# New instruction orders for all engines of a four-layer attention and gated-MLP kernel, with the loads in another order

## The chip, the cores and the metric

The kernel runs on one core of one Trainium2 chip. The metric is the device time of one execution in microseconds (us). One launch runs the whole program: two attention layers and two gated layers, alternating, with the activations kept in on-chip memory from the first load to the last store.

## The reference

The input x is 1 x 2048 x 448 in bf16. Cut to what matters, this is computed:

```python
def A(x, wqkv, wo):                       # 16 heads of 28
    q, k, v = split_heads(x @ wqkv)
    idx = pos[:, None] - (arange(8) * 2)[None, :]     # 8 keys, every second position back
    logits = where(idx >= 0, einsum("bhsd,bhswd->bhsw", q, k[idx]) * 28 ** -0.5, -1e9)
    o = einsum("bhsw,bhswd->bhsd", softmax(logits), v[idx])
    return merge_heads(o) @ wo

def B(x, w_gate, w_up, w_down):           # 448 -> 1792 -> 448
    return ((x @ w_gate) * (x @ w_up)) @ w_down

x = x + A(layernorm(x), A_wqkv, A_wo)
x = x + B(layernorm(x), B_w_gate, B_w_up, B_w_down)
x = x + A(layernorm(x), A_wqkv, A_wo)
x = x + B(layernorm(x), B_w_gate, B_w_up, B_w_down)
```

## The kernel before

**Tiling.** Tokens lie in 16 blocks of 128, even positions in blocks 0 to 7 and odd ones in 8 to 15, so that the dilated window of 8 becomes a plain window of 8 neighbours. A layer is cut into chunks: layer 0 into chunks of 256, 512, 512, 512 and 256 tokens (blocks 0-1, 2-5, 6-9, 10-13, 14-15), the others likewise. `SEQ` (line 99) gives the order in which attention chunks (A) and gated chunks (B) are set up.

**Operations.** `build` adds 1592 numbered operations to a `Sched`. Each has the engines that may run it, its instructions, the keys it waits for and the PSUM banks that it takes or gives back. The number is the order in which `build` adds them, and the same number means the same operation before and after the change. What the text below names:

- 0 and 1 load the two halves of the first x block group (blocks 0-1 and 2-3), 6, 11 and 12 the other x groups (four blocks each); 7 and 8 load the V weights, 2 to 5 the four row pieces of the Q and K weights into a staging area, 9 and 10 the V columns that later ride in the padding of the Q and K weights (all in `load_x` and `plain_dma`, line 440).
- 13 loads ScalarE's function table; 14 (`c_warm`) clears the operand of the warm-up products, 16 (`c_wo`) clears `wo_g`.
- 46 to 61 are 16 warm-up products that keep TensorE busy with zeros.
- 62 to 69 copy the staged Q and K weights into `WQK` with each head padded from 28 to 32 columns (line 518); 70 to 77 fill the padding with V columns (line 526), which may only be done when the Q and K products of chunks 0 and 1 are finished.
- 99 to 196 are layer 0's layer norm, for each block B: statistics (line 579), aggregate (581), logarithm and exponential on ScalarE (582, 584), the normalised block `xn` (600), its transpose on TensorE (610, 614), and the copy `T` out of PSUM into `xnTa` (621, 624).
- 197 to 208 are Q and K of chunk 0 and their copies (line 709), 227 to 238 those of chunk 1, 349 to 360, 495 to 506 and 570 to 579 those of chunks 2, 3 and 4. 209 to 212 are V of query block 0, 239 to 242 V of query blocks 1 and 2, and so on.
- Scores S (832), their exponential (841), mask (848), the attention product AV (866), its copies and normalisation (877 to 904), and the output product Y (in `y_blocks`), whose result is added to x (921), are for one or two query blocks at a time: 214, 219 for block 0; 248, 253 for blocks 1 and 2; 270, 275 for 3 and 4; and so on.
- In a gated chunk, 14 units of gate and up products (`Gps`, `Ups`) are followed by a copy of the gate on ScalarE (957) and the product of both on VectorE (960); two passes of down products (`Dd`) follow, and the result is added to x.

**Products in halves.** The 448-deep products are cut in pieces of 64 rows; two pieces run at once in the two row halves of the array. `crossed` cuts a unit in two parts: in the second part the two outputs change row halves, and it waits for the first part's last product (`selfd`). Other units stand between the parts in the order, or none.

**Bursts.** S and AV are 64 (for query block 0, 32) short products in tiles of 64 x 32. An entry `248*2/350` in the order of TensorE says that operation 248 is cut in three, and two steps of unit 350 stand in between, each as eight products of 32 columns (line 350); the rest of 350 follows.

**The order.** Nothing is decided at run time. `ORDER` (line 101) lists, for each engine, the operations in the order in which they are issued; `BANKS` says which of the eight PSUM banks each operation takes. `Sched.schedule` reads both, and adds a wait for the operation that gives a bank back. `emit` writes one instruction stream for each engine, with a semaphore wait only where an operation needs another engine's result or a DMA. "sp" is the queue on which nearly all DMAs are issued, in order; a DMA that waits holds back all behind it. ScalarE issues two of the first loads on its own queue.

The few lines of the old order that matter here (the beginning of each list):

```python
"pe":  "46 ... 61 108 111 203 201 204 199 129 202 200 126 209 197 210 135 198 239 132 240 231 ..."
"act": "4 13 5 63 62 67 101 105 102 106 109 112 117 118 208 123 124 207 127 206 136 205 ..."
"dve": "14 16 44 15 45 99 103 100 104 64 65 68 107 110 113 115 114 116 121 119 128 ..."
"sp":  "7 0 3 8 10 2 11 9 1 6 12 79 80 78 81 82 ..."
```

So the loads go out as V weights, half of x, a Q and K piece, V weights, and so on, with two Q and K pieces on ScalarE's queue beside them; VectorE copies three of the Q and K weight pieces ahead of the first normalised block; and TensorE begins with Q and K of chunk 0.

Of the kernel before, what the change touches and what calls it, by code (L numbers as in the profile page):

```python
# [93 lines left out]
def grp_nc(g):  # L94
# [8 lines left out]
        "46 47 48 49 50 51 52 53 54 55 56 57 58 59 60 61 108 111 203 201 204 199 129 202 200 126 209 197 210 135 198 239 132 240 231 233 232 229 234 156 230 "  # L103
        "174 159 227 214 228 183 195 192 153 219 150 570 574 571 353 575 177 349 354 248*2/350 351 352 355 568 356 253*3/569 243 180 244 495 368 496 270*2/369 "
        "265 499 266 500 275*2/572 372 573 373 501 378 502 497 498 287 288 383 514 304 515 307 310 316 328 319 331 395 301 396 313 325 337 322 334 340 343 "
        "400*3/344 345 525*3/346 441 444 450 405*2/453 530*2/456 468 480 465 417 477 418 587 542 462 543 474 588 447 547*2/459 471 519 489 520 490 598*3/483 "
        "491 552*2/492 664 676 603*2/484 688 670 682 694 485 486 592 615 593 616 661 620*2/673 685 697 667 625*2/700 754 564 755 565 735 758 736 759 737 741 "
        "738 742 637 739 638 740 679 691 828 703 764*1/704 825 705 706 837 778*2/840 709 710 849 783+769*3/711 712 895 822 834 846 858 896 976 897 917 898 918 "
        "988 1000 852 979 819 893 899 894 900 985 795 997 1012 1009 991 1003 1015 796 912 831 843 855 982 994 913 867 868 1018 923*3/869 870 861 928*2/862 1006 "
        "863 864 1019 1034 945*3/1020 1046 940 1021 950*2/941 1058 1070 1043 1037 1040 1123 1108 1124 1109 1106 962 1107 963 1049 1061 1073 1128 1055 1129 1110 "  # L110
        "1104 1111 1105 1052 1064 1067 1076 1077 1134*2/1197 1078 1079 1209 1156*2/1206 1218 1275 1279 1276 1280 1139*2/1200 1161*2/1294 1212 1224 1281 1295 "
        "1282 1203 1215 1151 1173 1221 1233 1152 1230 1299 1174 1300 1227 1277 1236 1278 1247 1248 1239 1249 1310*3/1250 1240 1401 1395 1407 1398 1404 1241 "
        "1332*3/1242 1419 1315*2/1413 1337*2/1431 1304 1425 1416 1428 1327 1410 1328 1422 1349 1434 1350 1445 1446 1305 1437 1354*3/1438 1447 1448 1439 "
        "1359*2/1440 1476 1488 1473 1485 1371 1497 1509 1372 1479 1491 1503 1482 1494 1506 1500 1512 1544 1556 1515 1516 1541 1553 1565 1517 1518 1550 1523 "
        "1524 1547 1559 1571 1562 1574 1568 1580 1577 1525 1526 1589 1583 1586"
    ),
    "act": (
        "4 13 5 63 62 67 101 105 102 106 109 112 117 118 208 123 124 207 127 206 136 205 133 241 242 147 189 148 190 165 237 166 141 171 238 172 236 160 142 "
        "216 215 235 184 221 151 577 579 178 224 359 249 250 225 358 360 255 576 181 262 258 263 259 503 272 271 370 371 505 276 277 295 578 296 374 284 280 "
        "285 281 379 380 504 506 385 384 305 425 516 426 308 392 388 311 389 393 317 320 329 332 302 314 326 431 323 432 338 335 341 402 401 527 526 442 445 "  # L120
        "451 719 720 406 407 454 532 414 457 410 415 411 469 539 481 540 535 466 536 478 463 645 646 475 589 448 548 651 460 652 549 472 521 600 599 553 554 "
        "665 561 557 562 558 677 877 689 878 671 612 683 613 608 695 609 594 725 726 662 621 622 809 674 810 686 698 668 627 626 701 634 756 635 630 631 743 "
        "760 803 804 744 680 692 970 829 971 766 765 826 838 779 883 841 884 780 850 770 785 788 789 823 835 1088 1089 774 847 775 859 902 792 977 793 919 989 "
        "1001 853 980 820 904 986 998 1013 1010 992 1004 1016 832 1028 1029 844 856 983 914 995 924 925 1259 1260 1007 933 937 934 938 1035 946 1094 947 1095 "
        "1047 951 952 1059 1044 955 1071 1038 956 1041 959 960 1181 1125 1182 1114 1113 1265 1266 1050 1062 1074 1187 1056 1188 1130 1115 1053 1065 1068 1136 "
        "1135 1198 1210 1157 1158 1207 1219 1283 1140 1201 1162 1144 1145 1148 1213 1149 1166 1167 1225 1170 1286 1171 1204 1216 1222 1234 1231 1379 1301 1380 "
        "1228 1237 1385 1386 1311 1312 1402 1396 1408 1399 1405 1334 1333 1420 1317 1414 1338 1324 1339 1325 1320 1432 1321 1426 1346 1347 1417 1342 1429 1343 "
        "1411 1423 1457 1435 1458 1306 1463 1464 1356 1355 1361 1360 1477 1364 1368 1365 1369 1489 1474 1486 1498 1510 1480 1492 1535 1536 1504 1483 1495 1507 "
        "1501 1513 1545 1557 1542 1554 1566 1551 1548 1560 1572 1563 1575 1569 1581 1578 1588"
    ),  # L130
    "dve": (
        "14 16 44 15 45 99 103 100 104 64 65 68 107 110 113 115 114 116 121 119 128 120 122 125 130 137 131 134 163 145 169 164 187 146 161 185 138 143 186 170 "
        "144 188 167 162 139 155 140 158 168 211 213 173 157 212 175 182 191 194 149 152 218 72 196 217 193 154 179 176 220 247 222 223 269 357 251 252 226 254 "
        "256 261 257 245 246 264 260 377 274 273 268 267 293 291 294 292 278 283 279 299 297 399 286 282 381 382 290 289 423 421 386 424 422 391 306 387 433 "
        "309 435 312 390 394 318 321 330 333 303 398 397 429 427 315 428 430 327 324 439 339 336 342 437 524 404 403 546 348 347 717 528 443 529 718 715 446 "
        "716 452 727 408 413 455 409 531 458 533 416 412 538 470 534 482 541 467 537 420 419 479 643 641 644 642 464 545 653 649 544 476 647 650 655 449 648 "
        "597 550 461 659 551 473 657 619 729 602 601 494 555 493 560 556 666 873 875 605 876 678 559 874 604 563 690 606 611 672 607 684 614 696 610 488 487 "
        "723 721 724 722 618 617 807 733 805 663 806 731 808 623 624 675 687 817 815 699 885 669 628 633 702 629 567 566 801 799 802 632 636 800 811 813 746 "
        "640 639 745 968 763 966 969 887 681 967 693 830 972 777 768 767 827 708 707 881 879 882 839 880 781 842 891 889 782 851 784 771 786 974 787 713 714 "
        "1084 1086 790 1087 824 772 1085 773 836 1096 1098 848 776 791 860 978 794 903 990 1002 854 981 821 901 922 987 999 1014 1011 993 1005 798 797 1026 "  # L140
        "1024 1027 1017 1025 833 1030 1032 845 857 984 996 944 926 927 872 871 1257 1255 1258 930 1256 929 931 932 936 1008 866 865 939 1092 1090 1036 1091 "
# [961 lines left out]
```

## Time and profile before

| what | value |
|---|---|
| time, median of 3 runs (lowest, highest) | 389.65 us (388.76, 390.45) |
| the profiled execution | 389.88 us |
| its span (first to last instruction) | 388.2 us |
| matmuls on TensorE | 6592 |
| granted TensorE clock in the span | 0.999 |
| DMA moved | 22.53 MB, mean 58 GB/s |
| DMA in the first slice of 9.7 us | 276 GB/s |

The page shows an engine's busy time as a share of the span, and the chain of waits followed back from the end. The windows give the same busy times for stretches of the span. In the timeline each row is a run of instructions of one kind: start, time, engine, line, operation, what it writes and reads, how many; in brackets how long the engine stood idle before it and what ended that. TensorE has two rows of its own: PE for products, PEld for weight loads, which overlap the products.

### The profile page before, as it was taken

The numbers are of one execution on the slowest core, as the hardware profiler recorded it, in microseconds if no ns is written. First come the engines' busy times: TensorE is split into PE (matmuls) and PEld (weight loads), VectorE is DVE, ScalarE is ACT, GpSimd is POOL, SyncE is SP. The second block draws the span as 40 slices with busy tenths as digits, with TensorE's granted clock in tenths as the row PEclk, the third lists the DMA queues.
The fourth block names the chain that finished last, engine by engine and source line by source line (L and its number), as shares of the span: only waits on it lengthen the run. The fifth ranks groups of instructions, "written<-read, shape, count | busy, mean of one in ns | idle before, by whom it ended". The sixth has DMA issues, their size and how long they took to land.

```text
span 388.2 us, 14856 instructions
## 1 busy us (share of the span) xinstructions
PE 377.8 (97%) x6592; PEld 210.9 (54%) x6592; DVE 286.6 (74%) x635; ACT 206.9 (53%) x393; POOL 8.7 (2%) x40
## 2 busy tenths in 40 slices
PE   6899999999999999999999999999999999999997
PEld 2554557554554454555665666645444545544674
DVE  4996798789878898678574889659685788666342
ACT  3788895674664572446343456458324573444230
POOL 7010000000000000000000000000000000000000
PEclk9999999999999999999999999999999999999999
DMA  8767533210420243221012014720042104502001
GB/s 276 179 154 169 147 68 63 53 22 8 79 37 3 30 63 74 41 52 29 5 24 51 2 31 63 89 54 3 2 94 50 34 3 48 99 2 47 3 25 49
DMA packets 54867, 22.53 MB, mean 58 GB/s; under 512 B 44996, under 2 KB 54804, under 8 KB 54804
## 3 DMA queue, kind: packets, MB, share of 16 engines
q1 hardware_dynamic: 54372, 21.08, 26.8%
q8 instruction: 52, 0.85, 0.9%
q10 hardware_dynamic: 432, 0.52, 0.4%
q14 instruction: 11, 0.09, 0.1%
HBM read 8.54 MB, written 2.71 MB: 29 GB/s over the span
## 4 chain that ended last, share of the span: by engine, by line
PE 91%; DVE 4%; DMA 1%; SPq 1%; issue 1%; POOL 0%; ACT 0%; POOLq 0%; DVEq 0%
PE ps L347 82%; PE ps L350 4%; PE ps L866 2%; PE ps L832 2%; DVE st L579 2%; PE ps L972 1%; DMA x_sb<-in_A_x_dram 1%; SPq L440 1%; DVE xn_sb L600 1%; DVE oT L904 0%; DVE R_sb L891 0%; POOL WQK L526 0%; DVE mv L581 0%; DVE Qz L820 0%; ACT O_sb L877 0%
## 5 line engine op out<-in xcount | busy, mean ns | idle before, releaser
L347 PE MATMUL ps<-xnTb,WGU 64*128 64x512 bf16 (+1 forms) x1916 | 174.7, 332 | 0.0
L347 PEld LDWEIGHTS ps<-xnTb,WGU 64*128 64x128 bf16 x1916 | 92.3, 94 | 70.9 <-DVE x_sb L921 0.8
L957 ACT ACTIVATE g_sb<-ps 128x512 bf16<-128x512 f32 (+1 forms) x140 | 71.2, 510 | 93.8 <-PE ps L347 71.6
L960 DVE TENSOR_TENSOR hT<-g_sb,ps 128x512 bf16<-128x512 bf16 (+1 forms) x140 | 80.1, 575 | 43.9 <-ACT g_sb L957 42.2
L347 PE MATMUL ps<-WD,hT 64*128 64x448 bf16 x768 | 78.5, 349 | 0.1
L347 PE MATMUL ps<-xnTa,WQK 64*128 64x512 bf16 (+1 forms) x490 | 54.3, 354 | 1.1 <-ACT xnTa L621 0.9
L347 PEld LDWEIGHTS ps<-WD,hT 64*128 64x128 bf16 x768 | 36.2, 94 | 32.7 <-PE ps L347 0.5
L841 ACT ACTIVATE E_sb<-ps,shift_sb 128x1024 bf16<-128x1024 f32 (+1 forms) x36 | 37.0, 1071 | 24.9 <-PE ps L832 24.9
L921 DVE TENSOR_TENSOR x_sb<-x_sb,ps 128x448 bf16<-128x448 bf16 x62 | 35.9, 616 | 12.1 <-PE ps L347 11.9
L579 DVE BATCH_NORM_STATS2 st<-x_sb 128x6 f32<-128x448 bf16 x64 | 37.3, 613 | 3.5 <-DMA x_sb<-in_A_x_dram 3.5
L600 DVE TENSOR_SCALAR xn_sb<-x_sb,mv,rstd 128x512 bf16<-128x512 bf16 (+1 forms) x64 | 34.8, 571 | 2.9 <-DMA xnTb<-xn_sb 1.7
L347 PEld LDWEIGHTS ps<-xnTa,WQK 64*128 64x128 bf16 x490 | 22.7, 94 | 22.9 <-PE ps L347 1.1
L709 ACT ACTIVATE qk<-ps 128x1024 bf16<-128x1024 f32 (+1 forms) x28 | 25.1, 903 | 10.1 <-PE ps L347 10.0
L347 PE MATMUL ps<-wo_g,oT 64*128 64x448 bf16 x252 | 29.0, 349 | 0.6 <-DVE oT L904 0.5
L848 DVE TENSOR_TENSOR E_sb<-E_sb,MK 128x1024 bf16<-128x1024 bf16 (+1 forms) x36 | 23.8, 665 | 6.9 <-ACT E_sb L841 6.6
L820 DVE TENSOR_SCALAR Qz<-qk,qmask 128x960 bf16<-128x960 bf16 (+1 forms) x36 | 14.7, 452 | 16.2 <-PE ps L832 15.4
L347 PE MATMUL ps<-WV,xnTa 64*128 64x336 bf16 (+3 forms) x244 | 23.4, 303 | 0.0
L891 DVE STREAM_SHUFFLE R_sb<-O_sb 128x480 f32<-128x480 f32 (+1 forms) x34 | 23.2, 696 | 0.0
L904 DVE TENSOR_TENSOR oT<-O_sb,R_sb 128x480 bf16<-128x480 f32 (+3 forms) x36 | 21.7, 625 | 1.5 <-ACT R_sb L893 1.4
L892 ACT ACTIVATE R_sb<-R_sb 128x480 f32<-128x480 f32 (+1 forms) x34 | 20.1, 603 | 4.2 <-DVE R_sb L891 4.0
L893 ACT ACTIVATE R_sb<-R_sb 128x480 f32<-128x480 f32 (+1 forms) x34 | 19.7, 600 | 0.2
L347 PEld LDWEIGHTS ps<-wo_g,oT 64*128 64x128 bf16 x252 | 11.8, 94 | 13.1 <-DVE oT L904 1.3
(66 smaller groups left out, 230.7 us busy)
## 6 DMA issues: line engine op xcount, KB each, us to landing
out_dram<-x_sb SPq DMA_DIRECT2D x15, 112.0 KB, 1.7
x_sb<-in_A_x_dram SPq DMA_DIRECT2D x3, 448.0 KB, 5.6
WGU<-in_B_w_gate_dram SPq DMA_DIRECT2D x4, 224.0 KB, 3.7
WGU<-in_B_w_up_dram SPq DMA_DIRECT2D x4, 224.0 KB, 3.7
WD<-in_B_w_down_dram SPq DMA_DIRECT2D x2, 448.0 KB, 4.7
WGU<-in_B_w_gate_dram SPq DMA_DIRECT2D x2, 336.0 KB, 4.4
WGU<-in_B_w_up_dram SPq DMA_DIRECT2D x2, 336.0 KB, 5.3
WD<-in_B_w_down_dram SPq DMA_DIRECT2D x2, 336.0 KB, 5.5
```

Source lines behind the costliest of these rows:

```text
L347: return lambda E: E.matmul(out(), lhs(), rhs(), start=start, stop=stop)
L579: sc.add("dve", one(lambda E, B=B: E.bn_stats(st6[:, B, :], x_sb[:, B, :]), ("bn", li, B)), 525.0, deps=[("x", li - 1, B)] + ([("xn", li - ...
L600: sc.add("dve", one(lambda E, B=B, dst=dst, src=src: E.tensor_scalar(dst, src, mv[:, B, 0:1], rstd[:, B:B + 1], ALU.subtract, ALU.mult), ( ...
L709: return E.activation(dst, src, ACT.Copy) if hasattr(E, "activation") else E.tensor_copy(dst, src)
L841: return E.activation(E_sb[:, slot, 2 * hp:2 * hp + 2, 0:w], ps[:, b0:b0 + 2, 0:w], ACT.Exp, bias=shift_sb[:, 0:1], scale=SCALE)
L848: return E.tensor_tensor(e, e, MK[:, kind, 0:nc].unsqueeze(1).unsqueeze(1).to_broadcast([128, 2, w // nc, nc]), ALU.min)
L891: sc.add("dve", one(lambda E: E.stream_shuffle(R_sb[:, rs, 0:w], O_sb[:, os_, 0:w], [DH] * 32), ("Rs", li, qb)), dve_est(w) + 20.0, deps=[ ...
L892: sc.add("act", one(lambda E: E.activation(R_sb[:, rs, 0:w], R_sb[:, rs, 0:w], ACT.Ln), ("Rl", li, qb)), act_est(w, False), deps=[("Rs", l ...
L904: return E.tensor_tensor(oT[:, :, a % HALF:a % HALF + z - a], O[:, :, a - tok:z - tok], R_sb[:, rs, 0:w].rearrange("p (h n) -> p h n", h=4 ...
L921: sc.add("dve", one(lambda E: E.tensor_tensor(x_sb[:, B, :], x_sb[:, B, :], ps[:, bk[w], 0:D], ALU.add), ("x", li, B)), dve_est(D), deps=[ ...
L957: sc.add("act", one(lambda E, gs=gs, bk=bk: E.activation(g_sb[:, gs, 0:nt], ps[:, bk[0], 0:nt], ACT.Copy), ("G", li, j, fc)), act_est(nt), ...
L960: sc.add("dve", one(lambda E, gs=gs, bk=bk, fc=fc: E.tensor_tensor(hT[:, fc, hs, 0:nt], g_sb[:, gs, 0:nt], ps[:, bk[1], 0:nt], ALU.mult), ...
```

## The change

Only the two tables `ORDER` and `BANKS` are replaced. The operations, their numbers, shapes, data and dependencies stay. Every list gets a new order, on all five engines and over all four layers, and nearly all PSUM banks are dealt out anew. The lists were found with the loads modelled as one queue. The beginnings of the lists, cut:

```diff
     "pe": (
-        "46 47 48 49 50 51 52 53 54 55 56 57 58 59 60 61 108 111 203 201 204 199 129 202 200 126 209 197 210 135 198 239 132 240 231 233 232 229 234 156 230 "
-        "174 159 227 214 228 183 195 192 153 219 150 570 574 571 353 575 177 349 354 248*2/350 351 352 355 568 356 253*3/569 243 180 244 495 368 496 270*2/369 "
-        "265 499 266 500 275*2/572 372 573 373 501 378 502 497 498 287 288 383 514 304 515 307 310 316 328 319 331 395 301 396 313 325 337 322 334 340 343 "
...
+        "46 47 48 49 50 51 52 53 54 55 56 57 111 108 58 59 60 61 126 209 129 210 239 132 135 240 197 203 198 204 233 201 234 199 202 227 150 200 228 156 229 "
+        "231 159 230 183 232 153 177 214 174 353 192 180 351 195 352 248*2/354 574 575 349 219 350 253 495 497 498 496 570 243 571 270*2/244 499 500 265 266 "
+        "355 275*2/501 572 356 502 573 568 569 368 378 369 372 373 310 304 307 383 301 287 313 288 316 325 319 322 337 395 328 514 396 515 331 334 400 340 343 "
+        "525*3/344 345 346 530 405*2/587 519 588 520 441 444 447 417 459 450 418 462 456 471 542 453 543 474 547 465 477 468 480 552*2/483 592 484 593 485 667 "
...
     "act": (
-        "4 13 5 63 62 67 101 105 102 106 109 112 117 118 208 123 124 207 127 206 136 205 133 241 242 147 189 148 190 165 237 166 141 171 238 172 236 160 142 "
...
+        "13 5 4 105 106 101 102 117 118 66 109 112 123 127 124 62 65 133 136 241 242 212 208 141 205 165 142 238 147 207 166 148 206 171 235 172 157 189 160 "
+        "190 236 237 216 215 193 196 250 249 359 579 255 224 225 254 504 503 258 262 259 263 272 271 505 246 277 276 295 296 360 506 578 280 281 379 380 371 "
...
     "dve": (
-        "14 16 44 15 45 99 103 100 104 64 65 68 107 110 113 115 114 116 121 119 128 120 122 125 130 137 131 134 163 145 169 164 187 146 161 185 138 143 186 170 "
...
+        "15 16 14 103 99 104 115 100 113 116 110 114 107 119 125 121 120 122 128 139 130 131 134 69 140 137 161 211 163 167 143 162 138 168 164 44 145 169 146 "
+        "144 149 170 187 185 188 155 151 173 45 158 186 213 182 152 176 184 191 70 154 76 178 72 179 175 194 181 247 218 358 217 252 251 220 221 222 223 269 "
...
     "pool": (
-        "21 19 22 17 43 23 18 34 27 24 38 25 28 31 29 32 26 33 66 69 35 39 36 40 37 41 30 42 20 76 74 77 71 70 75 73"
+        "23 27 34 38 39 20 28 17 19 18 43 22 21 67 68 63 24 64 25 35 26 36 31 29 30 71 73 77 75 74 32 33 40 41 42 37"
     ),
     "sp": (
-        "7 0 3 8 10 2 11 9 1 6 12 79 80 78 81 82 83 84 85 86 87 88 89 91 94 90 92 93 95 367 362 365 361 364 366 363 96 97 375 98 376 517 586 584 582 300 298 "
...
+        "0 1 6 8 7 3 2 11 12 79 9 10 80 81 82 83 84 85 86 87 88 94 92 91 93 89 78 90 95 298 300 508 513 361 366 509 363 507 96 367 365 585 510 512 586 511 362 "
...
 BANKS = (
-        "46:0 108:1 111:0 126:23 129:01 132:23 135:23 150:45 153:67 156:45 159:23 174:45 177:01 180:67 183:23 192:45 195:67 197:45 199:67 201:45 203:23 209:01 "
...
+        "46:0 108:2 111:1 126:45 129:23 132:45 135:23 150:01 153:45 156:67 159:45 174:67 177:67 180:67 183:67 192:45 195:67 197:45 199:23 201:67 203:23 209:67 "
...
```

In words, at the beginning: x goes out first on SP's queue (0, 1, 6), then the V weights (8, 7), then two Q and K pieces (3, 2), then the rest of x (11, 12) between the first gated weights and the padding columns; the other two Q and K pieces stay on ScalarE's queue (5, 4). VectorE copies one Q and K weight piece (69) instead of three, after the normalised block 5; POOL copies four (67, 68, 63, 64), ScalarE three (66, 62, 65). TensorE runs 12 of its warm-up products, the transposes of blocks 1 and 0, the other four, and then V of query block 0 (209, 210) and of 1 and 2 (239, 240), with transposes between, before the first Q and K product (197). The padding copies (70 to 77) go to POOL but for three (70, 76, 72). At the end of the last layer the three last products are 1583, 1586, 1589 instead of 1589, 1583, 1586. Of the S and AV bursts of all layers, ten stand without a host unit instead of four, and 57 host steps stand between bursts instead of 71.

## The prediction

> **What bounds the kernel now.** I read the page's busy times first, then a table of windows, the timeline of the first 60 us, and the chain of waits.
>
> ```profile
> PE 377.8 (97%) x6592; PEld 210.9 (54%) x6592; DVE 286.6 (74%) x635; ACT 206.9 (53%) x393; POOL 8.7 (2%) x40
> ...
> PE 91%; DVE 4%; DMA 1%; SPq 1%; issue 1%; POOL 0%; ACT 0%; POOLq 0%; DVEq 0%
> ```
>
> TensorE is busy for 97% of the span and is 91% of the chain. A new order changes the time only by what TensorE waits, and by how closely its products are packed. The windows show where it waits (columns: stretch, its length, then busy us and instructions of PE, PEld, DVE, ACT, POOL).
>
> ```profile
> 0.00:10.00 10.00, 6.33 (x24) 2.43 (x24) 4.57 (x18) 3.92 (x9) 7.12 (x33) 1.00 0.85 280
> 10.00:20.00 10.00, 8.94 (x146) 5.81 (x148) 10.00 (x32) 8.03 (x21) 0.00 (x0) 1.00 0.69 172
> 20.00:30.00 10.00, 9.10 (x212) 5.10 (x209) 9.09 (x31) 8.74 (x18) 1.59 (x7) 1.00 0.61 152
> 30.00:40.00 10.00, 9.05 (x244) 4.81 (x242) 6.63 (x14) 8.61 (x13) 0.00 (x0) 1.00 0.74 156
> ...
> 50.00:60.00 10.00, 9.42 (x182) 5.81 (x180) 9.28 (x23) 9.30 (x18) 0.00 (x0) 1.00 0.35 66
> ...
> 220.00:230.00 10.00, 9.51 (x282) 6.81 (x278) 8.40 (x21) 4.62 (x10) 0.00 (x0) 1.00 0.14 30
> ```
>
> The idle time is 3.7 us in the first 10, 3.6 from 10 to 60, 0.5 near 226, and 2.4 after the last product. From 60 to 385 there is nothing else to win. From 10 to 30 us VectorE is full (10.00 and 9.09) and ScalarE nearly so: they feed TensorE, and what delays VectorE delays all. The first rows:
>
> ```profile
> 5.73 1.15 DVE L579 BATCH_NORM_STATS2 st<-x_sb 128x6 f32<-128x448 bf16 x2 [3.17 <-DMA x_sb<-in_A_x_dram]
> ...
> 8.61 0.92 DVE L600 TENSOR_SCALAR xn_sb<-x_sb,mv,rstd 128x512 bf16<-128x512 bf16 x2
> ...
> 9.88 1.15 DVE L579 BATCH_NORM_STATS2 st<-x_sb 128x6 f32<-128x448 bf16 x2 [0.36 <-DMA x_sb<-in_A_x_dram]
> ...
> 10.84 1.59 PE L347 MATMUL ps<-xnTa,WQK 64*128 64x256 bf16 x26 [0.86 <-ACT xnTa L621]
> ```
>
> VectorE gets the first half block of x at 5.73 and the second only at 9.88; TensorE's first products (Q, K) start at 10.84.
>
> To compare packing I take a product's column time at the full clock: 64 rows by n columns cost n/4.8 ns, since two halves run together (512 columns: 107 ns; 34 of them took 3.83 us in the timeline, 113 each). Summed over all products but the warm-up's, this is 350.0 us. So 38.2 us of the span are not column time. This loss stands at 16.1 us by 39.6, 18.0 by 52 and 19.4 by 56.
>
> **The head, part by part.** *Loads.* By 5.73 four loads of 224 KB had landed (896 KB), by 9.88 2352 KB: 351 KB/us. In the new order x's two halves and the next x block lead SP's queue, and ScalarE's queue still carries two QK weight pieces beside them. So x's first half is among the first 448 KB: 5.73 - 448/351 = 4.45. The second half 5.73, x block 1 7.0, V weights 8.3, the last QK piece 9.55. These are estimates from those two rows. Bounds: 4.1 (ScalarE's first load had landed when its copies began at 4.08) and 5.7 (x's first half as now).
>
> *VectorE.* With 0.575 per statistics, 0.15 per aggregate, 0.39 per normalisation (rows above), the new order gives xn of block 1 at 7.65 and of block 0 at 8.2; now both are done at 9.53. ScalarE copies their transposes (0.55 each) to 9.4 and 9.95.
>
> *TensorE.* V of query block 0 can start at 9.45, 1.4 earlier than now. But its second half stands behind the transpose of block 3, whose xn comes at 10.35; V of blocks 1 and 2 needs block 2's copy (10.9), and its second half stands behind the transposes of blocks 4 and 5 (12.1). Q and K then start at 13.4, their last weight copy (VectorE, operation 69) being done at 12.4. At that point 28 V products are done (1.96 us of columns) and six transposes; now, at the same time, 36 QK products (1.95) and three transposes. Gain: 0.3 of the 1.4. The warm-up starts 0.8 later, as its memset now stands behind the 0.81 of wo_g's, and still ends before 7, under cover of the wait for x.
>
> *To 40 us.* I followed the lists by hand, each instruction at its row's duration: QK copies 0.60 and 1.01, transposed copies 0.60 (ScalarE) or 0.42 (VectorE), score copies (L841) 1.07, masks 0.67. VectorE is without a break from 4.45 to 28, as it is now to 27. TensorE waits 0.55 before the first scores (block 7's copy comes behind a weight copy that waits for the last QK product of chunk 1), 0.15 at block 10, and 0.3 at the first AV. The padding copies on POOL, which now hold TensorE up at 25 to 26 (1.59 of POOL from 24.75), finish at 25.5, just before they are wanted. At 39.6 the loss is 15.6 against 16.1 now: 0.5 gained.
>
> *40 to 56.* Waits I find: 0.3 before the first Y, 0.55 for V of blocks 3 and 4 (ScalarE reaches its copy at 43.4, as number 64 of its list), 0.6 for V of blocks 7 and 8 before the AV of 5 and 6. Six units there have their second half straight behind the first. Such a half waits for the other's end. Today's second Y shows the price:
>
> ```profile
> 52.93 1.93 PE L347 MATMUL ps<-wo_g,oT 64*128 64x448 bf16 x16 [0.45 <-DVE oT L904]
> ...
> 53.92 0.49 PEld L347 LDWEIGHTS ps<-wo_g,oT 64*128 64x128 bf16 x8 [0.50 <-PE ps L347]
> ```
>
> The second half begins 0.99 after the first, whose columns take 0.75: 0.24. Six of them cost 1.4 (today three stand there). The loss comes to 19.2 at 52 and 19.8 at 56, against 18.0 and 19.4: today's own waits from 50 to 54 (0.56, 0.94 before Y) are not met, since Y now lies 6.8 and 9.1 us of columns behind its AV, where it is 4.6 and 4.7 today. **Head: +0.4.** Bounds: -1.4 (the whole early start kept, no new wait) to +1.9 (x as late as now: the 1.3 that VectorE starts earlier lost, and 0.2 on the way).
>
> **Bursts.** The score and AV products are short ones in bursts of 64; the lists let a host unit's 32-column strips in between. Four bursts stand without a host today, ten in the new list; five of these are behind 56 us, where today has none. The price from two rows:
>
> ```profile
> 46.03 0.27 PE L866 MATMUL ps<-E_sb,v_sb 64*32 64x64 bf16 x21
> ...
> 49.07 0.68 PE L832 MATMUL ps<-Qz,qk 64*32 64x64 bf16 x64
> ```
>
> The burst at 49.07 keeps TensorE 0.62 until the next product at 49.69. The one at 46.03 ends at 46.78 with 16 strips in between that are worth 0.21 of columns: 0.54. Difference about 0.1, times five: **+0.5** (0 to 1).
>
> **Bank and chain distances behind 56.** Between what TensorE must wait for and its next use, the new list leaves about as many us as today's: 3.3 from scores to AV (today 3.3; needed: two score copies 2.14 and a mask 0.67), 2.6 from Q/K to scores in one place (today 4.9; needed 1.03 and 0.85). **0**, up to +1 where ScalarE is late.
>
> **Tail.** The last three groups of products have 448, 224, 224 columns instead of 224, 448, 224. The last addition and store are the same 0.39 and a 56 KB store, now from SP instead of ScalarE. **0** (0.1 either way).
>
> **Stops without a waiter.** Two idle times of TensorE have no releaser:
>
> ```profile
> 37.43 0.88 issue
> ...
> 226.37 0.49 issue
> ```
>
> Counting its weight loads, products and own waits in the timeline, they come before number 1217 and number 8385: 28 times 256 apart, inside a burst's or a transpose's instructions. So I read them as TensorE waiting for its next 256 instructions; 49 other such borders cost 0.2 or nothing. The new list meets as many borders. **0**, with bounds -1.4 (none) and +1.8 (two more at 0.9). The Trainium skill (Runtime: NRT & Kernel Launch, section Instruction fetch mechanics) says that instructions come in blocks of 256 and that a border is mostly hidden. The block size agrees with the 28 times 256; "mostly hidden" agrees with 49 of 51 borders. By that rule alone the price of a border would be nothing, and the third rival below would fall.
>
> **Sum.** 0.4 + 0.5 = +0.9 on the profiled execution's 389.88 us (span 388.2 and 1.7 around it): 390.8. That execution is 0.23 above the median of 389.65, so against the median I expect **390.6**. About 0.5% (1.9 us) is what can be told from no change; 390.6 is within it (387.7 to 391.6).
>
> **Rivals.**
> *A, the early start is kept.* For: VectorE, full from 10 to 28, begins 1.3 earlier, and what it does first comes out first. Against: it carries the same work, and V's halves stand behind late transposes. Price: -1.4 at the start, and today's waits from 50 to 54 saved (-1.5): 389.65 - 2.9 = 386.8. Chance 0.22.
> *B, x comes late.* VectorE's third statistics are those of block 3, in x's second half, and everything of blocks 0 and 1 stands behind them. Should that half land with block 1 of x (7.0, if SP's loads share the engines rather than follow each other), VectorE stands still for 1.3, which nothing hides up to 28 us, and the sum is 390.6 + 1.3 = 391.9. It decides from a landing at 6.8 on. For: in the rows loads near each other land within 0.7. Against: 351 KB/us fits the landings in between. Further waits of this kind from 40 to 56, where ScalarE is busy 0.9 of the time, come on top: to 394. Chance 0.22.
> *C, more stops at borders.* Three pairs of bursts are back to back in the new list (AV of 9 to 10 and 7 to 8 in layer 0, and two in layer 2), where today has one: 256 instructions in some 1.3 us, the shortest time between two borders now being 3.4. Two more stops of 0.9: 392.4. Against: 49 of 51 borders cost next to nothing. Chance 0.13.
> *Forecast,* the changes cancel: 0.43, its own range 388.6 to 391.6.
>
> So faster by over 0.5%: 0.22; within: 0.43; slower: 0.35. The range runs from 387.0 (half of A is left out) to 394.0 (what lies beyond B and C).
>
> **What will show it.** VectorE's first statistics at 4.4, its third without a wait; the first V product near 9.5 and the first QK product near 13.4, not before 12.5. The loss at 39.6 near 15.6, at 56 near 19.8. Waits before the first Y and the AV of 3 and 4. Wrong if x's second half lands after 6.8, if TensorE's idle time from 10 to 60 is below 2 or above 6 us, or if idle time without a releaser is over 3 us in all.

## The result, and the profile after

The changed kernel ("after") takes **390.81 us** (median of 19 runs, 389.97 to 392.35); before, beside it on the same chip, takes 389.38 us (19 runs, 388.11 to 390.90). The ratio is 1.0033, 95% interval 1.0021 to 1.0044: 0.8 to 1.7 us slower. The profiled execution of after took 391.03 us with a span of 389.3 us. The forecast was 390.6. The total is right, but by luck: terms behind it are wrong and cancel.

Part of what the two medians differ by is not the orders. In the runs below, before was executed 71 times, and its time goes with its granted clock: median 388.8 us at 1.00 (21 executions), 389.6 at 0.996 (36), 390.6 at 0.991 (14). After ran at 1.00 in all of its 25 executions, here and in a2. At the same clock it is slower by about 2.0 us (this result against that 388.8) to 2.7 us (a2 against before's three at 1.00 on its chip), not by 1.4.

All of after's lines stand one lower in its file (L347 is now L348). Its page, busy times and chain:

```profile
PE 379.0 (97%) x6508; PEld 212.8 (55%) x6508; DVE 290.3 (75%) x640; ACT 203.2 (52%) x388; POOL 9.7 (2%) x40
...
PE 90%; DMA 3%; DVE 3%; ACT 2%; issue 1%; SPq 0%
```

TensorE is still the bound. DMA has gone from 1% to 3% of the chain: transfers now end waits of TensorE. The windows of after:

```profile
0.00:10.00 10.00, 6.95 (x38) 2.67 (x38) 6.40 (x19) 4.56 (x12) 4.62 (x21) 1.00 0.83 277
10.00:20.00 10.00, 9.75 (x158) 6.13 (x158) 9.46 (x37) 9.22 (x24) 2.65 (x10) 1.00 0.75 175
...
30.00:40.00 10.00, 9.69 (x254) 5.04 (x254) 8.52 (x19) 8.96 (x15) 0.00 (x0) 1.00 0.62 159
40.00:50.00 10.00, 9.77 (x234) 5.26 (x230) 8.29 (x21) 8.34 (x14) 0.00 (x0) 1.00 0.26 50
50.00:60.00 10.00, 8.68 (x194) 6.89 (x194) 8.16 (x20) 7.37 (x16) 0.00 (x0) 1.00 0.57 159
60.00:70.00 10.00, 10.00 (x228) 7.30 (x232) 9.54 (x24) 6.12 (x14) 0.00 (x0) 1.00 0.16 32
70.00:80.00 10.00, 8.64 (x298) 5.13 (x270) 9.73 (x21) 5.80 (x11) 0.00 (x0) 1.00 0.41 78
220.00:230.00 10.00, 10.00 (x126) 6.09 (x122) 8.78 (x23) 4.99 (x10) 0.00 (x0) 1.00 0.16 28
```

TensorE is busier than before in the first 20 us (6.95 and 9.75 against 6.33 and 8.94). From 30 to 40 it is busier too (9.69 against 9.05), but there 0.88 of before's idle time is the stop at 37.43 that the prediction shows. TensorE loses 1.3 us from 50 to 60 and 1.4 from 70 to 80. VectorE is nearly full from 60 to 80 (9.54 and 9.73; before it had 8.88 and 8.03 there).

To see where the time went, I gave each product in the two traces to its operation. At some points of the two lists exactly the same products are behind. There the two times can be compared. The last two columns do the same with e5 (below), which runs before's lists but for the warm-up products and whose trace has no stop without a releaser:

| the same work is done at | after, us | before, us | after minus before | e5, us | after minus e5 |
|---|---|---|---|---|---|
| layer 0, before the scores of blocks 7 and 8 | 66.98 | 68.13 | -1.15 | 67.38 | -0.40 |
| down product of chunk (1,0) done | 74.55 | 75.52 | -0.97 | 74.77 | -0.22 |
| layer 1, among the gate and up products of its fourth chunk | 152.1 | 151.6 | +0.5 | 151.1 | +1.0 |
| layer 3, among those of its first chunk | 243.2 | 242.9 | +0.3 | 241.8 | +1.5 |
| layer 3, later | 331.4 | 330.2 | +1.2 | 329.2 | +2.2 |
| the last group of products but two | 381.4 | 380.1 | +1.3 | 379.2 | +2.2 |

Against before's trace the head (the part up to 67 us) gains 1.0 to 1.15 us. But most of that is before's stop at 37.43, which belongs to that one execution: e6 (below) runs the same list of products without it, and its distance behind before falls from 2.79 to 1.83 us at just this product. What the new orders gain in the head is 0.2 to 0.4 us, by e5. The stretch from 75 to 152 costs 1.2 to 1.5, that from 152 to 331 another 1.2 against e5 (before's second stop, 0.49 at 226.37, hides part of it, and after has two small stops near 295). TensorE's larger waits in the timeline of after, as far as 80 us:

```profile
23.12 0.33 PE L833 MATMUL ps<-Qz,qk 64*32 64x80 bf16 x32 [0.56 <-DVE WQK L527]
...
25.04 0.82 PE L348 MATMUL ps<-xnTa,WQK 64*128 64x512 bf16 x6 [0.22 <-ACT E_sb L842]
...
30.32 0.32 PE L867 MATMUL ps<-E_sb,v_sb 64*32 64x72 bf16 x32 [0.18 <-ACT E_sb L842]
...
52.11 2.47 PE L348 MATMUL ps<-xnTb,WGU 64*128 64x256 bf16 x42 [1.26 <-ACT R_sb L893]
...
79.33 2.98 PE L348 MATMUL ps<-xnTb,WGU 64*128 64x512 bf16 x26 [1.30 <-DMA xnTb<-xn_sb]
```

The two large waits stand in front of the first gate and up products of chunks (1,0) and (1,1), which read `xnTb`, written by transposing transfers. (The row at 52.11 names ScalarE's R, which that product doesn't need. In experiment e4 the same wait, 1.55 us at 53.68, names the transfer.) The first of them takes most of what is left of the lead by then: by column time after is 1.2 us ahead of e5 at 46 us and 0.3 at 57. For the wait at 79.33, the way back on VectorE and SyncE in after:

```profile
66.85 0.71 DVE L601 TENSOR_SCALAR xn_sb<-x_sb,mv,rstd 128x896 bf16<-128x896 bf16 x1
...
70.25 0.71 DVE L601 TENSOR_SCALAR xn_sb<-x_sb,mv,rstd 128x896 bf16<-128x896 bf16 x1
...
71.48 1.38 DVE L601 TENSOR_SCALAR xn_sb<-x_sb,mv,rstd 128x896 bf16<-128x896 bf16 x2
...
67.59 4.77 SPq L604 DMA_TRANSPOSE xnTb<-xn_sb  x2
72.92 3.16 SPq L604 DMA_TRANSPOSE xnTb<-xn_sb  x2
```

Four token blocks are needed. VectorE makes the row of block 3 at 66.85 and then turns to other work. The rows of blocks 2, 4 and 5 come at 70.25 to 72.86. SyncE's queue holds the second transfer until 70.96 (the end of block 2's row), the last one is issued by 76.08, and the product that waits for it begins at 79.33. Before, the same four transfers and the product behind them, which does not wait:

```profile
59.55 1.85 SPq L603 DMA_TRANSPOSE xnTb<-xn_sb  x1
...
62.72 1.30 SPq L603 DMA_TRANSPOSE xnTb<-xn_sb  x1
...
69.11 2.87 SPq L603 DMA_TRANSPOSE xnTb<-xn_sb  x2
...
75.52 2.75 PE L347 MATMUL ps<-xnTb,WGU 64*128 64x512 bf16 x24
```

### The profile page after: what moved, and what is told of

It reads as the page before. It is cut to its first block, busy times and chain, and to the rows that moved or that the text cites. A ratio compares the mean times of both kernels' runs of the same rounds, so it can differ in the third digit from the quotient of the medians.

```text
span 389.3 us, 14648 instructions
## 1 busy us (share of the span) xinstructions
PE 379.0 (97%) x6508; PEld 212.8 (55%) x6508; DVE 290.3 (75%) x640; ACT 203.2 (52%) x388; POOL 9.7 (2%) x40
## 4 chain that ended last, share of the span: by engine, by line
PE 90%; DMA 3%; DVE 3%; ACT 2%; issue 1%; SPq 0%
PE ps L348 82%; PE ps L351 3%; PE ps L833 2%; PE ps L867 2%; ACT E_sb L842 2%; PE ps L973 1%; DMA x_sb<-in_A_x_dram 1%; DMA xnTb<-xn_sb 1%; DMA xnTa<-xn_sb 1%; DVE xn_sb L601 1%; DVE st L580 1%; DVE E_sb L849 0%; PE ps L615 0%; ACT g_sb L958 0%; ACT v_sb L802 0%
## 5 line engine op out<-in xcount | busy, mean ns | idle before, releaser
L348 PE MATMUL ps<-xnTb,WGU 64*128 64x512 bf16 (+1 forms) x1944 | 177.7, 333 | 2.6 <-DMA xnTb<-xn_sb 1.3
L348 PEld LDWEIGHTS ps<-xnTb,WGU 64*128 64x128 bf16 x1944 | 94.9, 94 | 76.0 <-DMA xnTb<-xn_sb 1.6
L958 ACT ACTIVATE g_sb<-ps 128x512 bf16<-128x512 f32 (+1 forms) x140 | 69.6, 509 | 102.4 <-PE ps L348 87.7
L961 DVE TENSOR_TENSOR hT<-g_sb,ps 128x512 bf16<-128x512 bf16 (+1 forms) x140 | 77.9, 574 | 48.0 <-ACT g_sb L958 44.2
L348 PE MATMUL ps<-WD,hT 64*128 64x448 bf16 x766 | 79.0, 350 | 0.5 <-issue 0.3
L348 PEld LDWEIGHTS ps<-WD,hT 64*128 64x128 bf16 x766 | 36.1, 94 | 32.8 <-issue 1.3
L348 PE MATMUL ps<-xnTa,WQK 64*128 64x512 bf16 (+1 forms) x488 | 52.5, 352 | 0.5 <-ACT E_sb L842 0.2
L922 DVE TENSOR_TENSOR x_sb<-x_sb,ps 128x448 bf16<-128x448 bf16 x62 | 36.8, 614 | 11.8 <-PE ps L348 11.7
L580 DVE BATCH_NORM_STATS2 st<-x_sb 128x6 f32<-128x448 bf16 x64 | 38.4, 615 | 2.9 <-DMA x_sb<-in_A_x_dram 2.5
L348 PEld LDWEIGHTS ps<-xnTa,WQK 64*128 64x128 bf16 x488 | 22.8, 94 | 20.5 <-PE ps L348 1.8
L348 PE MATMUL ps<-wo_g,oT 64*128 64x448 bf16 x256 | 29.2, 349 | 0.1
L710 ACT ACTIVATE qk<-ps 128x1024 bf16<-128x1024 f32 (+1 forms) x25 | 22.4, 920 | 8.6 <-PE ps L348 8.3
L348 PE MATMUL ps<-WV,xnTa 64*128 64x336 bf16 (+3 forms) x244 | 22.5, 304 | 0.1
L878 ACT ACTIVATE O_sb<-ps 128x512 f32<-128x512 f32 (+2 forms) x22 | 11.9, 562 | 17.3 <-PE ps L867 17.2
L348 PEld LDWEIGHTS ps<-wo_g,oT 64*128 64x128 bf16 x256 | 12.4, 94 | 11.8 <-PE ps L348 0.5
```

Source lines behind the costliest of these rows:

```text
L348: return lambda E: E.matmul(out(), lhs(), rhs(), start=start, stop=stop)
L580: sc.add("dve", one(lambda E, B=B: E.bn_stats(st6[:, B, :], x_sb[:, B, :]), ("bn", li, B)), 525.0, deps=[("x", li - 1, B)] + ([("xn", li - ...
L710: return E.activation(dst, src, ACT.Copy) if hasattr(E, "activation") else E.tensor_copy(dst, src)
L922: sc.add("dve", one(lambda E: E.tensor_tensor(x_sb[:, B, :], x_sb[:, B, :], ps[:, bk[w], 0:D], ALU.add), ("x", li, B)), dve_est(D), deps=[ ...
L958: sc.add("act", one(lambda E, gs=gs, bk=bk: E.activation(g_sb[:, gs, 0:nt], ps[:, bk[0], 0:nt], ACT.Copy), ("G", li, j, fc)), act_est(nt), ...
L961: sc.add("dve", one(lambda E, gs=gs, bk=bk, fc=fc: E.tensor_tensor(hT[:, fc, hs, 0:nt], g_sb[:, gs, 0:nt], ps[:, bk[1], 0:nt], ALU.mult), ...
```

## The experiments

Each time stands beside that of before, measured together with it on the same chip. The kernels built on after keep its operations and change its lists alone, except where code is shown.

**h1 and h2: the two halves changed over.** h1 runs after's lists to the point "66.98 / 68.13" of the table and before's behind it; the point is called the joint below. h2 runs before's lists to there and after's behind. h1 also has one move on SyncE's list:

```diff
-436 ... 434 ... 440 438
+436 434 440 438
```

> The orders of after up to 67 us (the point at which both kernels have done exactly the same products: 67.0 us in the trace of after, 68.1 in that of before), and the orders of before behind it; three of SyncE's issues (434, 440, 438) are moved up behind 436. Theory 1, the head gains and the middle gives it back: the 1.1 us stays gained, 388.3 against 389.4 for before and 390.8 for after; no wait over 0.3 us at the first gate and up products of chunk (1,1). Rival, the head's gain is lost again whatever follows, because VectorE and the transposing transfers are behind by then: 389.4 to 390.5, with the wait of some 1.3 us near 76 us as in after.

> The other half: the orders of before up to 68.1 us, the orders of after behind it. Theory 1: the middle and the rest of after cost 1.5 to 75-152 us and 0.9 to 243-331 us against before, so the time is 389.4 + 2.3 = 391.7. If the wait of 1.30 us on the transposing transfers near 78 us comes only from work that the head of after had put off, it is absent here and the time is 390.4. Rival, the head is what costs: 389.4 or less.

h1: 391.41 us against 389.2 (ratio 1.0037, 1.0014 to 1.0061). h2: 393.82 against 389.2 (1.0100, 1.0065 to 1.0135). Neither is near 389, and every expected time is missed, h1's by 0.9 and h2's by 2.1 us at least. In h1 TensorE does arrive early against before's trace (its loss at 66 us is 19.0, before's 19.9 with the stop of 0.88 in it), and then:

```profile
68.50 1.70 PE L349 MATMUL ps<-xnTb,WGU 64*128 64x256 bf16 x28 [1.82 <-DVE hT L962]
...
71.81 0.26 PE L834 MATMUL ps<-Qz,qk 64*32 64x64 bf16 x16 [0.28 <-DVE hT L962]
```

The lead is gone at once, in a wait for VectorE's H, which frees the bank. This is not the wait that either theory named. It can be the joint's own doing, so h1 by itself decides nothing; h3 goes on from it. h2 has the same kind of wait at its joint (1.01 us, also for H) and loses another 2.5 us behind it in its trace. Of these, 1.85 are two stops without a releaser (0.83 at 82.89, 1.02 at 295.53), where before has one of 0.49. So after's second part costs about 1.1 more than before's in these traces once the stops are left out. h2 also lost 1.9 us in its first 24 us, where its lists are those of before: the clock, below.

**e3: the rows for the transfers earlier.**

```diff
 "dve"
-427 428 435 333 336 524 342 429 430 433 404 437 439
+427 429 428 430 435 433 333 336 524 342 437 439 404
 "act"
-341 402 431 432
+341 431 432 402
```

> After with VectorE's statistics and normalized rows for the transfers T(1,2) to T(1,5) moved some places earlier (and ScalarE's two steps for them). Theory 1: the wait of 1.30 us at 78 us in front of the first gate and up products of chunk (1,1) is gone or below 0.4; what is put off on VectorE (9.5 to 9.7 tenths busy there) takes back up to 0.5; the time is 389.5 to 390.3, 0.5 to 1.3 below after. Rival, that wait only took in what the later stops and bursts would cost anyway: the time stays at 390.8, with new idle time of about 1 us in the 20 us behind.

390.13 against 389.2 (1.0014, 0.9994 to 1.0035). The wait at 78 us is gone: no idle time over 0.1 us from 70 us to the end. But a new one has come 10 us earlier, in the down product, since H comes later by what was moved up:

```profile
69.99 1.50 PE L349 MATMUL ps<-WD,hT 64*128 64x448 bf16 x14 [1.00 <-DVE hT L962]
```

The time is in theory 1's range, but 1.00 of the 1.30 is given back, where 0.5 was expected. In the traces e3 is level with after from 80 to 175 us, 0.2 ahead from there to 290 and 1.07 at the end. The 0.87 arises at two products near 292 and 298, where after stops and e3 does not (below, at a2); the list of products is the same. So the edit's own share is at most 0.2 us.

**e8 and e6: the load order alone.** e8 is after with the loads of before; e6 is before with the loads of after.

```diff
 e8 "sp"
-0 1 6 8 7 3 2 11 12 79 9 10 80
+7 0 3 8 10 2 11 9 1 6 12 79 80
 e8 "act"
-13 5 4
+4 13 5
 e6 "sp"
-7 0 3 8 10 2 11 9 1 6 12 79
+0 1 6 8 7 3 2 11 12 9 10 79
 e6 "act"
-4 13 5
+13 5 4
```

> After with the load order of before alone (SyncE's first twelve issues and ScalarE's first three). Theory 1, the engines' new orders need x first: x's second half lands at 9.5 to 9.9 instead of 6.0, VectorE stops in front of the third statistics, the first product of V moves from 9.3 to 13 to 13.5, and the time is 390.8 + 3.8 = 394.6. Rival, the first products of Q and K can take the place of V because the weights are there sooner: their order is fixed, so only 1 to 2 us are lost, 392 to 393.

> Before with the load order of after alone (SyncE's first issues and ScalarE's three). Theory 1, the loads and the orders go together: VectorE starts 1.1 us earlier on x, but the first products are still those of Q and K, whose last weight piece lands near 9.5 and is copied behind the normalizations; the first product of Q and K comes at 11.3 to 12.5 instead of 10.84, and the time is 389.4 + 0.5 to 1.7 = 390 to 391. Rival, x first is the gain by itself: 388.3 or less.

e8: 395.4 against 389.2 (1.0143, 1.0106 to 1.0179). e6: 391.8 against 389.45 (1.0061, 1.0039 to 1.0084). The waits of TensorE for the first normalised rows, in e8 and then in e6:

```profile
11.49 1.03 PE L612 MATMUL ps<-ident,xn_sb 128*128 128x128 bf16 x8 [5.06 <-DVE xn_sb L602]
```

```profile
11.03 0.72 PE L612 MATMUL ps<-ident,xn_sb 128*128 128x128 bf16 x8 [4.15 <-DVE xn_sb L602]
```

After waits 0.60 there, before 2.39. Theory 1 of e8 holds, 0.8 us above its time: e8's wait is 4.46 longer than after's, and its trace is 4.5 behind after's at the end (5.0 at the first V product). Its clock was halved from 10 to 14 us as well (below), so the wait is not the only cost. The new orders need the early x, and in e6 the early x by itself gains nothing. In e6 VectorE's list still has copies of the Q and K weights ahead of the rows, and these weights now land last: VectorE stands still for 3.56 us in front of those copies. The time is 0.8 over the upper end expected; the clock (below) fell to 0.77 from 10 to 14 us there too, and all twelve executions of e6 ran below 1.00.

**e4 and f1: hosts for seven bursts.** f1 is e3 with 433 moved behind 342 on VectorE's list, and with the same seven hosts.

```diff
-219 350 / 253 495 / 378 369 / 383 301 / 400 340 / 547 465 / 764 705
+219*2/350 / 253*2/495 / 378*2/369 / 383*2/301 / 400*2/340 / 547*2/465 / 764*2/705
```

> After with seven bursts of short products that stand without a host given their next unit as host (219, 253, 378, 383, 400, 547, 764, each with two pieces let in). Theory 1: a burst without a host lost 0.37 to 0.47 us in the trace of after, one with two pieces 0.32; seven times 0.1 gives 390.8 - 0.7 = 390.1. Rival, the host's pieces wait for transfers or banks inside the burst, or the burst's reader is late by as much: 390.6 to 391.0.

> After with both repairs: VectorE's rows for the transfers T(1,2) to T(1,5) earlier (as in e3, with the one of T(1,2) behind the last H of chunk (1,0), so that the down product waits 0.3 us and not 1.0), and the seven hosts. Theory 1: both add up, 390.1 - 0.5 - 0.7 = 389.0. Rival, they aren't worth more together than alone: 390.

e4: 392.19 against 389.45 (1.0063, 1.0036 to 1.0090). f1: 392.90 (1.0094, 1.0060 to 1.0128). The ratios of after are 1.0033 and, in its second run (a2, below), 1.0053: by the medians e4 is 0.4 to 1.2 us slower than after instead of 0.7 faster, though the intervals overlap. f1 is 2 us slower than f2 (below), which is f1 without hosts, and those intervals do not overlap. Both are above what even the rivals expected. In the timeline of e4 two of the hosted bursts wait:

```profile
56.69 0.28 PE L868 MATMUL ps<-E_sb,v_sb 64*32 64x64 bf16 x21 [0.55 <-ACT g_sb L959]
...
69.61 0.29 PE L834 MATMUL ps<-Qz,qk 64*32 64x64 bf16 x20 [0.47 <-ACT g_sb L959]
```

A host needs its two banks when the burst begins, and ScalarE has not yet emptied them. In after the burst (54.51, 0.68 us) runs without a wait while ScalarE does it. A third waits 0.29, at 99.9 us. Here a burst without a host is 0.1 us dearer and saves a wait of 0.3 to 0.55. f1 shows the same three waits (0.55, 0.47, 0.29). But e4 also has two stops without a releaser, and f1 two at the same products (0.25 and 0.53):

```profile
37.80 0.61 PE L349 MATMUL ps<-xnTa,WQK 64*128 64x256 bf16 x8 [0.82 <-issue]
```

```profile
79.39 0.28 PE L868 MATMUL ps<-E_sb,v_sb 64*32 64x64 bf16 x22 [0.64 <-issue]
```

The strips make 168 more instructions on TensorE, so other products stand at such places. How much of the lost time is the hosts' waits and how much the stops, no run separates.

**e5: the instruction numbers moved.** Before, with more and narrower warm-up products (the edit put in short):

```diff
-one product of 512 columns for each of the last three warm-ups
+for q in range(8): E.matmul(ps[:, bank, 0:64], warm[:, 0:128], warm[:, 0:64])
```

> Before with its last three warm-up products each made of eight products of 64 columns: 21 products, 42 instructions more on TensorE ahead of all the work, and a shorter gap without products before the first transposes. Theory 1, the waits without a releaser (0.88 us at instruction 1219, 0.49 at 8385, both 193 to 195 above a multiple of 256) belong to the instruction number: none at those products, others at 193 to 195 above a multiple of 256, which is now 42 instructions earlier in the work; the time within 0.5 us of before, 388.7 to 389.7. Rival, they belong to those products (a bank, a semaphore): they stay at the same products, now at 235 to 237 above a multiple of 256.

389.88 against 389.45 (1.0011, 0.9989 to 1.0033). The stops at the two products are gone, and no other without a releaser is over 0.1 us at a border: neither theory in full. e6, with before's numbers unchanged, has no such stop either, so e5 alone does not show that the number decides; the places of all the stops together speak for it (last section). The profiled execution was e5's fastest, 388.94, and the median is that of before, so a stop more or less is within what varies from one execution to the next.

**a2: after again; f2: e3 with H first.**

```diff
 f2 "dve", against e3
-435 433 333 336 524 342 437 439
+435 333 336 524 342 433 437 439
```

> After, unchanged, beside the repairs on one chip. Theory, the wait at 78 us comes from the order and the stops at 292 and 298 us from the chip's fetching of instructions: the wait of 1.2 to 1.4 us in front of the first products of chunk (1,1) is there again, the idle times at 292 and 298 may be another length or absent; 390.8. Rival, both belong to the order: all three are there again at the same lengths.

> As e3, but VectorE makes the last H of chunk (1,0) before the normalized rows for T(1,2). Theory: the down product at 69 us waits 0.3 us where it waited 1.0 in e3, the wait at 78 us stays gone (below 0.4), and the time is 389.4 to 389.9, 1.0 below a2. Rival, the row for T(1,2) is now so late that the first products of chunk (1,1) wait for it again, by 0.7: 390.1 to 390.5.

a2: 391.54 against 389.62 (1.0053, 1.0038 to 1.0068). f2: 390.88 (1.0034, 1.0017 to 1.0051). In a2:

```profile
79.18 3.19 PE L348 MATMUL ps<-xnTb,WGU 64*128 64x512 bf16 x27 [1.21 <-DMA xnTb<-xn_sb]
```

The wait at 78 us is there again; idle time where after stopped at 292.24 (0.14) and 298.07 (0.28) is not, and a2's trace gains 0.4 on after's in that place. Product by product, against e3, after loses 0.29 and 0.54 at these two products and a2 still 0.20 and 0.27. So the wait belongs to the order, and the length of the stops changes from one execution to the next. In f2 both waits are there, each smaller:

```profile
69.24 1.50 PE L349 MATMUL ps<-WD,hT 64*128 64x448 bf16 x14 [0.35 <-DVE hT L962]
...
79.57 1.69 PE L349 MATMUL ps<-xnTb,WGU 64*128 64x512 bf16 x14 [0.68 <-DMA xnTb<-xn_sb]
```

The rival of f2 was right about the wait (0.68 for 0.7), and its time is 0.4 above that rival's range. From 67 to 80 us after waits 1.30 us, e3 1.00, f2 1.03: VectorE's list decides where the wait stands more than whether there is one.

**h3: h1 with a smooth joint.** Against h1: VectorE's list is f2's up to the joint, and the lists and banks behind are set right.

```diff
 "dve"
+333 433 336 342 439 437 524 404 403
 "act"
+426 335 341 431 432 402 401
 "sp"
+436 584 582 434 581 580 583 440 438 523 522
 banks of the second part
+0->2 1->3 2->0 3->1 4->6 5->7 6->4 7->5
```

> As h1 (the orders of after to 67 us, those of before behind), with a smooth joint: VectorE's statistics as in e3, its last two H of chunk (1,0) ahead of other work, ScalarE's gates and SyncE's transposing transfers to match, and the banks of the second part renamed to those that come free first. Theory, the head's gain of 0.8 to 1.1 us is real and the joint was what h1 lost (1.82 + 0.28 us of waits for H there): wait at the joint below 0.6, a wait of up to 0.7 for T(1,4) and T(1,5) behind it, 388.6 to 389.2. Rival, the head has run ahead of VectorE, and whatever stands next waits: 389.8 or more, with 1 us or more of idle time between 66 and 78 us.

395.29 against 389.62 (1.0146, 1.0129 to 1.0162). At the joint TensorE is 0.91 us ahead of before; then come three waits:

```profile
68.72 0.94 PE L349 MATMUL ps<-xnTb,WGU 64*128 64x256 bf16 x14 [1.33 <-DVE hT L962]
72.69 0.23 PE L834 MATMUL ps<-Qz,qk 64*32 64x80 bf16 x5 [1.01 <-issue]
79.70 2.74 PE L349 MATMUL ps<-xnTb,WGU 64*128 64x512 bf16 x12 [2.17 <-DMA xnTb<-xn_sb]
```

The rival holds: whatever stands next waits. For the second wait the profile names no releaser. How much of the 4.5 us is a bad joint and how much VectorE's lateness this run does not separate, and the last wait brings the clock down (below). The 0.91 itself is against before's trace; against e5 it is about 0.15, so there was hardly a lead to keep.

**f4: two rows on POOL.** Against f2:

```diff
-sc.add("dve", one(lambda E, B=B, dst=dst, src=src: E.tensor_scalar(
+sc.add(("dve", "pool") if (li, B) in ((1, 2), (1, 3)) else "dve", one(lambda E, B=B, dst=dst, src=src: E.tensor_scalar(
 "dve"
-433 435
 "pool"
+435 433
```

> As f2, but the normalized rows for T(1,2) and T(1,3) are made on POOL, which is idle from 30 us on, and not on VectorE. Theory, what holds the repaired kernels up between 67 and 80 us is VectorE's throughput (it has no break from 58 to 72 us there): 1.4 us less on VectorE takes away the 0.35 at 69 us and the 0.68 at 79 us, if POOL needs at most twice VectorE's 0.72 for a row (between 0.72 and four times that, 2.9, is what can be bounded); 389.9 and both waits below 0.2, 1.0 below f2. Rival 1, POOL needs over 2 us for a row, or holds VectorE up beside it: the transposing transfers come later than in f2, the wait at 79 us is 1 us or more, 391 or above. Rival 2, latency of the chain from the last sum of the residual to the transfer and not VectorE's load: the wait at 79 us stays 0.5 to 0.7, 390.5.

393.19 against 389.94 (1.0084, 1.0062 to 1.0105).

```profile
66.82 6.70 POOL L602 TENSOR_SCALAR xn_sb<-x_sb,mv,rstd 128x896 bf16<-128x896 bf16 x2 [41.63 <-ACT rstd L586]
...
80.44 1.90 PE L349 MATMUL ps<-xnTb,WGU 64*128 64x512 bf16 x16 [2.51 <-DMA xnTb<-xn_sb]
```

Rival 1: a row takes POOL 3.35 us, 4.7 times VectorE's 0.71, and the transfers are late by it. But with 1.4 us taken off VectorE the wait of 0.35 at 69 us is gone, and TensorE stands 0.94 ahead of f2 there. That VectorE's load makes that wait is so shown; that the wait at 79 us would have gone too is not. The profiled execution, 391.49, is the fastest of six; the four with a granted clock of 0.995 or 0.996 took 393.1 to 393.4.

No version beat before. e3 comes nearest, within its interval; at the full clock it is slower too: 389.64 to 391.57 in its twelve executions, 388.48 to 389.20 in before's nine on that chip.

## Why the prediction was right, and where it was not

*Loads and VectorE: right.* VectorE's first statistics came at 4.63 (4.45 was forecast), the third at 5.97 with no wait for a load, the row of block 1 by 7.56 (7.65). The second half of x had landed well before the 6.8 from which rival B decides: B is refuted. The first rows of VectorE and of the products in after:

```profile
4.63 1.15 DVE L580 BATCH_NORM_STATS2 st<-x_sb 128x6 f32<-128x448 bf16 x2 [2.46 <-DMA x_sb<-in_A_x_dram]
...
5.97 0.63 DVE L580 BATCH_NORM_STATS2 st<-x_sb 128x6 f32<-128x448 bf16 x1
...
9.33 0.45 PE L348 MATMUL ps<-WV,xnTa 64*128 64x224 bf16 x6
...
12.60 3.64 PE L348 MATMUL ps<-xnTa,WQK 64*128 64x256 bf16 x50
```

*TensorE's start: the gain was mis-sized.* "Gain: 0.3 of the 1.4" failed. The first V came at 9.33 (9.45 forecast), but Q and K at 12.60 and not 13.4: between the two TensorE stood idle for only 0.43. The loss was 9.7 at 13.4 us against 10.8 before, 1.1 better, and 1.8 better at 22 us.

*To 40 us: right but for that start.* The waits were 0.56, 0.22 and 0.18 where 0.55, 0.15 and 0.3 were forecast. The loss at 39.6 was 14.3, not 15.6; the difference is the start's. But the 16.1 of before, with which both are compared, holds the stop of 0.88; in e5 the loss there is 15.3. The forecast counted that stop's absence as a gain of the head and at the same time put the term for stops at 0.

*40 to 56: the three waits were not there; one that was not on the list was.* Before the first Y, for V of 3 and 4 and for V of 7 and 8 there is nothing over 0.1 us. Instead the first products of chunk (1,0) wait 1.26. No run took that wait away, so what it is worth is open. The loss at 56 was 18.4 and not 19.8. **Head +0.4** was in fact -1.0 to -1.15 against before's trace, inside its bounds (-1.4 to +1.9) and toward rival A; in h3, whose orders are the same nearly to there, it was -0.9. Against e5, without before's stop, it was -0.2 to -0.4: the early start is real at 27 us (about 2 us of columns ahead) and nearly used up by 57.

*Bursts +0.5: the price per burst held, its meaning is doubtful.* A burst without a host loses 0.37 to 0.47 us in after, one with two pieces 0.32: 0.1, as forecast. But in e4 and f1 hosts for seven of them gained nothing, so it is not shown that the old manner would have saved the 0.5 here.

*"Bank and chain distances behind 56: 0": this is the step that failed.* I followed the distances from scores to AV and from Q/K to scores, and not the chain from the residual's last sum through statistics, row and transposing transfer to the gate and up products. It costs 1.30 us at 78 (1.21 in a2) and 1.26 at 52. Moving VectorE's work took the wait at 78 away only by making another (1.00 in e3, 0.35 in f2), so the limit there is VectorE's list between 60 and 80 us. What after loses behind 152 us, some 1.2 us against e5, is in part its two stops and for the rest open.

*Stops 0: inside the bounds, but not 0.* Each of the two traces has two stops without a releaser, together 0.42 us in after and 1.37 in before: -0.95, by the luck of two executions; none over 0.1 in e3. Rival C, more stops in the new list, is not borne out by after's traces. The 0.9 us that after loses from 243 to 331 is partly of this kind: a2, the same kernel, has 0.4 of it back.

So the sum +0.9 met a measured +1.15 between the two profiled executions because a head 1.55 us better than forecast (-1.15 for +0.4) and a rest 1.8 us worse (+2.3 for +0.5) nearly cancel. The median of before agrees with its profiled execution by luck too: that one has 1.37 us of stops at a clock of 0.999, while 50 of the 71 others ran at a lower clock. The mechanism that was forecast, a head and bursts slightly dearer and nothing behind them, is not what happened.

## What to carry to other kernels

An earlier start is worth what the engines behind it leave over: some 2 us gained by 27 us were down to 0.2 to 0.4 by 75, and gone in the wait at 78, where VectorE was more than 9.5 tenths busy; moving its work moved the wait. Before a difference between two traces is given to the orders, take out the stops that no wait explains, and compare executions at the same granted clock: here these two were as large as the effect. When a new order is judged, follow every chain that ends in a product, transfers included, and not only those that wait today. A load order and the orders that it was made for belong together: each alone cost 2.4 (e6) and 6.2 us (e8), the lower clock included.

## What the runs showed of the hardware

**The granted clock can halve after a short gap.** Stretches of the windows of before, h2, e8 and h3; the third number from the end is the granted clock:

```profile
10.00:14.00 4.00, 2.94 (x64) 2.41 (x64) 4.00 (x13) 2.92 (x9) 0.00 (x0) 1.00 1.01 276
```

```profile
10.00:14.00 4.00, 3.31 (x39) 2.26 (x38) 3.12 (x10) 2.06 (x6) 0.00 (x0) 0.50 1.01 284
```

```profile
10.00:14.00 4.00, 2.51 (x12) 1.23 (x12) 4.00 (x14) 2.73 (x8) 0.00 (x0) 0.50 0.89 262
```

```profile
80.00:82.00 2.00, 2.00 (x12) 0.77 (x10) 0.00 (x0) 0.00 (x0) 0.00 (x0) 0.50 0.08 16
```

TensorE had been idle for 2.39 us (before), 2.03 (h2), 5.06 (e8) and 2.17 (h3) shortly ahead. h2 runs the lists of before there, and lost 1.9 us by 24 us. So gaps of 2.0 to 2.4 us may or may not bring the clock down. Before's own executions fit this: 21 of 71 kept 1.00, the others had 0.996 or 0.991 and took about 0.8 and 1.8 us more. Where in those the clock fell, no trace shows. After, with a gap of 0.60, kept 1.00 in all 25. The Trainium skill (TensorE: Matmul & The Clock Gate, section HAM oscillation — how this bites in real kernels) has the clock fall when TensorE idles longer than about 3.4 us. e8 agrees; h2 and h3 fell after less.

**Stops at borders of 256 instructions.** Counting TensorE's products, weight loads and own waits, stops without a releaser came at numbers 707, 1217, 1219, 3265, 3267, 4289, 8385, 10689, 10691 and 10947 in before, after, h1, h2, e8, e4 and f1, at 0.14 to 1.02 us each. All are 193 to 195 above a multiple of 256. Their places go by the number and not by the product: number 1217 to 1219 falls on a transpose in before and on a Q or K product in e4 and f1. And the stops come and go between executions: after and e8 stop at 10691 and 10947, while a2, e3, f2 and f4, with the same list of products, show no idle time there; before stops at 1217, e6 with the same list does not.

**POOL** takes 3.35 us for a normalised row of 128 x 896 that takes VectorE 0.71.
